# Attention and a feed-forward layer in fp32 on one core: the instruction plan redrafted with other transfer times and another table of moved works

## The chip, the cores and the metric

The kernel runs on one core of one Trainium2 chip. The metric is the device time of one execution in microseconds (us). Engines are named as the profile names them: PE multiplies matrices (PEld is its weight load), DVE and ACT do the elementwise work, SP issues every DMA; POOL only sets constants at the start.

## The reference, cut to what matters

```python
scores = scale * np.matmul(q, k.transpose(0, 1, 3, 2))          # 4 batches, 12 heads, 448 tokens, head size 64
scores = np.where(mask, -1000000000.0, scores)                  # causal
attn = np.exp(scores - np.max(scores, axis=-1, keepdims=True))
attn = attn / (np.sum(attn, axis=-1, keepdims=True) + 1e-09)
x = np.matmul(attn, v)                                          # then 1792 tokens x 768
...
h = x @ w_in                                                    # 768 -> 2048, w_in and w_out are float64
g = np.where(h > 0.0, h, np.exp(np.minimum(h, 0.0)) - 1.0)
return (g @ w_out).astype(np.float32)                           # 2048 -> 768
```

## The kernel before, in words

Attention goes by pairs of heads: 6 pairs for each of 4 batches. A pair's scores (L534, tile `sc`) are reduced to a masked, shifted block on DVE (L439, tiles `a` and `nm`), exponentiated on ACT (L443, with the row sums `su`), transposed on PE (L565, tile `tr`), copied out by ACT (L569) or DVE (L570, tile `at`), and multiplied with `v` on PE (L584, tile `av`). The sums become reciprocals on DVE (L448 and L449, tile `rr`). For the first two pairs of batch 0 the reciprocals `rr_80` and `rr_81` are spread over the partitions by PE (L604, tile `rb`) and copied by ACT (L871, tile `rs`); later ones go through a small DRAM round trip (`rdram`, `R`). DVE multiplies `av` with them (L608 or L466) into x.

The weights come as float64 bit patterns. Each piece of w_in (`w64`, 768 KB, L696) is turned into fp32 by five steps: DVE L704, ACT L708, DVE L709, ACT L712, DVE L715. It is then split into a high and a low part (`whl`: the high part on ACT L743 or DVE L744, the low part on DVE L746). A product of two such split operands is three matmuls (L785 to L787, hi·hi, hi·lo, lo·hi). The first two pieces of w_in are used unsplit (L808). The second batch group and most of the output layer use sums and differences of blocks (L751), so that seven block products do for eight.

The order of all of this is not that of the program text. Every step is recorded as a work with its engine (or two possible engines), a cost, a due time and what it reads and writes. `Plan.draft` then goes through time with a small model: it keeps one clock for each engine, a time `moved` until which the DMA engines are taken, and for each work the time at which it ends; at each turn it lets the earliest engine take, among the works that could start by then, the one that is wanted first. A work's wanted time is its due time less its entry in a table of numbers, `SOONER`, by the work's number: a positive entry makes it wanted earlier, a negative one later. `Plan.run` issues the instructions in the order that comes out. All engines work through their queues in that order, and real semaphores hold them back where something is not ready; the model's times only set the order.

For a transfer the model says when its data are there. Before, that is the end of the bytes' own time plus `LANDS`, 3.2, for a transfer that is issued after `CALM`, 75.0, and plus 1.3 for one issued earlier.

Of the kernel before, what the change touches and what calls it, by code (L numbers as in the profile page):

```python
# [108 lines left out]
class Plan:  # L109
# [9 lines left out]

    SOON = 20.0  # L120

    CALM = 75.0

    FAR, QUEUE = 1e9, 2.0

# [5 lines left out]
    def add(self, ways, reads=(), writes=(), due=None, size=0.0, hold=(), after=None):  # L131
# [24 lines left out]
        return w  # L156

    SOONER = {
# [50 lines left out]
    }  # L209

    def rank(self):
# [17 lines left out]
    def draft(self, shift):  # L229
# [14 lines left out]
        moved = 0.0  # L244
        ready = {w: 0.0 for w in self.works if not w.missing}
        order = []
        while len(order) < len(self.works):
            starts = {}
            for w, t in ready.items():
# [19 lines left out]
                for way, (eng, cost, _, port) in enumerate(w.ways):  # L269
                    s = max(t, free.get(eng, 0.0))  # L270
                    if w.size and w.want > s + self.FAR:
                        s = max(s, moved - self.QUEUE)
                    if port:
                        s = max([s] + [f for e, f in ported.items() if e != eng])
# [15 lines left out]
            s, _, _, way, w = min((c for c in cands if c[0] <= s0 + 0.12), key=lambda c: (c[1], c[2]))  # L290
            _, cost, fn, port = w.ways[way]
# [5 lines left out]
                    b.ring.order.append(b)  # L297
            free[eng], w.eng = s + cost, eng
            if w.size:
                moved = max(moved, s + cost) + w.size  # L300
                w.end = moved + (self.LANDS if s > self.CALM else 1.3)
            else:
                w.end = s + cost
            order.append((w, way, s, w.end))
# [886 lines left out]
```

## Time and profile before

| what | value |
|---|---|
| median of 3 runs | 602.02 us (600.16 to 603.22) |
| the profiled execution, its own time | 599.75 us |
| its span, first to last instruction | 598.0 us |
| PE, PEld, DVE, ACT busy share of the span | 98%, 87%, 86%, 73% |
| mean granted clock of PE | 0.994 of full speed |

The span and the 1.75 us around it make the profiled time. A busy PE means that a matmul is somewhere in its pipe; so a gap in PE is a true wait, but a busy PE may still be slowed. "Granted clock" is the share of PE's full clock: 1.00 is 2.4 GHz, 0.5 is 1.2 GHz.

### The profile page before, as it was taken

The page shows a single profiled execution, that of the slowest core. Times are in us where ns is not written, and L with a number is a line of the kernel's source. Part 1 is how long each engine was busy: PE and PEld are TensorE (multiplying, and loading weights), DVE is VectorE, ACT ScalarE, POOL GpSimd, SP SyncE. Part 2 cuts the span into 40 slices and gives each one's busy share as a digit, 9 for nine tenths or more (in the row PEclk, how much of TensorE's full clock was granted, in tenths as well). Part 3 has the DMA queues.
Part 4 walks back from the last instruction along what each step waited for, and adds up shares of the span by engine and source line. Part 5 has one row for each costly group of instructions (what it writes and reads, how often), then busy time and mean ns, then how long its engine had stood idle before and what let it go on. Part 6 is the DMA issues. An engine that isn't in the chain of part 4 may idle for free.

```text
span 598.0 us, 11375 instructions
## 1 busy us (share of the span) xinstructions
PE 586.7 (98%) x4010; PEld 519.4 (87%) x4010; DVE 515.3 (86%) x1234; ACT 435.8 (73%) x998; POOL 1.5 (0%) x12
## 2 busy tenths in 40 slices
PE   7799999999999999999999999999999999999998
PEld 4677798989889888888889989999999999999997
DVE  5698899998989899999998897999778999999452
ACT  6899999998888988998777876247464758764410
POOL 0000000000000000000000000000000000000000
PEclk9799999999999999999999999999999999999999
DMA  8995977768779999897456478999733242353112
GB/s 232 408 269 167 305 219 264 214 207 224 229 230 334 359 327 317 269 292 220 136 134 222 122 253 300 336 319 315 249 85 131 80 140 98 95 161 100 36 62 76
DMA packets 81976, 127.58 MB, mean 213 GB/s; under 512 B 9472, under 2 KB 58112, under 8 KB 81920
## 3 DMA queue, kind: packets, MB, share of 16 engines
q1 hardware_dynamic: 81920, 126.87, 67.0%
q8 instruction: 31, 0.51, 0.4%
q14 instruction: 25, 0.20, 0.1%
HBM read 94.63 MB, written 32.21 MB: 212 GB/s over the span
## 4 chain that ended last, share of the span: by engine, by line
PE 82%; DVE 9%; DMA 4%; ACT 2%; issue 1%; SPq 1%; DVEq 0%; ACTq 0%
PE hp L785 12%; PE hp L787 11%; PE hp L786 11%; PE op L785 10%; PE op L786 10%; PE op L787 10%; PE av L584 6%; PE tr L565 6%; PE sc L534 5%; DVE a L439 2%; DVE whl L746 2%; DVE G L751 1%; DMA w<-in_w_in 1%; DMA k<-in_qk 1%; PE hp L808 1%
## 5 line engine op out<-in xcount | busy, mean ns | idle before, releaser
L743 ACT ACTIVATE whl<-w 128x768 fp32r<-128x768 f32 x105 | 87.6, 838 | 64.6 <-PE op L787 31.3
L785 PE MATMUL op<-ph,whl 128*128 128x448 f32 (+1 forms) x338 | 125.4, 371 | 0.0
L786 PE MATMUL op<-pl,whl 128*128 128x448 f32 (+1 forms) x338 | 123.5, 365 | 0.1
L787 PE MATMUL op<-ph,whl 128*128 128x448 f32 (+1 forms) x338 | 123.4, 365 | 0.0
L443 ACT ACTIVATE a<-a,nm 112x448 f32<-112x448 f32 (+3 forms) x192 | 99.5, 522 | 30.6 <-DVE nm L439 30.4
L746 DVE TENSOR_TENSOR whl<-w,whl 128x768 fp32r<-128x768 f32 x111 | 104.3, 951 | 3.4 <-ACT whl L743 2.8
L439 DVE CUSTOM_DVE_ANT_0 a<-sc,mask 112x112 f32<-112x112 f32 (+3 forms) x192 | 76.2, 443 | 13.2 <-PE sc L534 12.9
L785 PE MATMUL hp<-xh,whl 128*128 128x448 f32 x180 | 70.3, 390 | 0.0
L785 PEld LDWEIGHTS op<-ph,whl 128*128 128x128 f32 x338 | 63.5, 188 | 5.9 <-issue 0.3
L786 PEld LDWEIGHTS op<-pl,whl 128*128 128x128 f32 x338 | 63.6, 188 | 5.6 <-DVE pl L746 1.0
L787 PEld LDWEIGHTS op<-ph,whl 128*128 128x128 f32 x338 | 63.5, 188 | 5.5 <-DVE whl L746 0.5
L787 PE MATMUL hp<-xh,whl 128*128 128x448 f32 x180 | 65.9, 366 | 0.4 <-DVE whl L746 0.4
L786 PE MATMUL hp<-xl,whl 128*128 128x448 f32 x180 | 65.8, 365 | 0.0
L785 PE MATMUL hp<-ph,whl 128*128 128x448 f32 x168 | 61.5, 366 | 0.0
L787 PE MATMUL hp<-ph,whl 128*128 128x448 f32 x168 | 61.4, 365 | 0.0
L786 PE MATMUL hp<-pl,whl 128*128 128x448 f32 x168 | 61.3, 365 | 0.0
L565 PEld LDWEIGHTS tr<-ident,a 112*112 112x112 f32 x480 | 50.0, 134 | 10.2 <-issue 3.1
L565 PE MATMUL tr<-ident,a 112*112 112x112 f32 x480 | 57.6, 263 | 0.0
L569 ACT ACTIVATE at<-tr 112x448 f32<-112x448 f32 x114 | 55.4, 536 | 3.0 <-PE tr L565 2.9
L584 PEld LDWEIGHTS av<-at,v 112*64 112x64 f32 x960 | 46.6, 138 | 6.5 <-issue 2.5
L584 PE MATMUL av<-at,v 112*64 112x112 f32 x960 | 51.7, 263 | 0.0
L746 DVE TENSOR_TENSOR pl<-G,ph 128x448 fp32r<-128x448 f32 x64 | 38.4, 617 | 3.9 <-ACT ph L743 3.6
(92 smaller groups left out, 941.6 us busy)
## 6 DMA issues: line engine op xcount, KB each, us to landing
w<-kin SPq DMA_DIRECT2D x41, 384.0 KB, 4.9
w<-in_w_in SPq DMA_DIRECT2D x16, 768.0 KB, 7.8
w<-in_w_out SPq DMA_DIRECT2D x24, 512.0 KB, 5.9
w<-sout SPq DMA_DIRECT2D x32, 384.0 KB, 3.8
w<-kout SPq DMA_DIRECT2D x24, 384.0 KB, 3.8
kin<-w SPq DMA_DIRECT2D x16, 384.0 KB, 6.0
sout<-w SPq DMA_DIRECT2D x12, 512.0 KB, 6.6
sin<-w SPq DMA_DIRECT2D x16, 384.0 KB, 3.9
```

Of the source, the lines that this page charges most:

```text
L439: plan.add(dve(n, lambda: nc.vector.tensor_tensor_reduce(out=a()[:, c], in0=sc()[:, c], in1=mask[:, S - n:], op0=ALU.add, op1=ALU.min, sca ...
L443: plan.add(act(n, lambda: nc.scalar.activation(a()[:, c], a()[:, c], AF.Exp, bias=nm()[:, x:x + 1], scale=-1.0, accum_out=su()[:, x:x + 1] ...
L534: nc.tensor.matmul(sc[half]()[:, lo:lo + n], q(d, x, i), k(d, y, n), start=j == 0, stop=j == len(split) - 1,)
L565: nc.tensor.transpose(tr()[:, chunk(x)], group["a"][half]()[:, chunk(x)], ident)
L569: act(w, lambda: nc.scalar.activation(at()[:, :w], tr()[:, :w], AF.Copy)),
L584: nc.tensor.matmul(av()[half_of(half), chunk(i)], u["v"]()[:, half, c], at()[:, chunk(x)], start=c == 0, stop=c == i,)
L743: act(n, lambda: nc.scalar.activation(h(), x(), AF.Copy), 0.09),
L746: sub = lambda eng: lambda: eng.tensor_tensor(out=l(), in0=x(), in1=f32(h()), op=ALU.subtract)
L751: two = lambda eng: lambda: eng.tensor_tensor(out=out(), in0=x(), in1=y(), op=op)
L785: nc.tensor.matmul(acc(), wh(k), xh(), start=first, stop=False, skip_group_check=more)
L786: nc.tensor.matmul(acc(), wh(k), xl(), start=False, stop=False, skip_group_check=more)
L787: nc.tensor.matmul(acc(), wl(k), xh(), start=False, stop=last, skip_group_check=more)
```

## The change

The model's transfers are described anew, and the table is another one. While the model's `moved` is before `BEGIN`, 14.0, a transfer's bytes take 1.35 times as long (`SLOWLY`); and every transfer lands `LANDS`, 3.2, after them, early or late. No work is added or taken away, and no size, buffer or cost of a work changes. The table has about as many entries as before, with other works and other numbers (its rows are cut here to one each). From line 302 on, lines of the changed kernel have a number that is higher by one (L704 before is L705 now).

```diff
-    CALM = 75.0
+    BEGIN, SLOWLY = 14.0, 1.35
...
     SOONER = {
-        21: -18.2, 27: -21.4, 29: -6.9, 32: 10.2, 37: -12, 56: 40.2, 62: -13.4, 85: -30.9, 106: 45.5,
+        12: -55.9, 54: -74.4, 55: -11.4, 87: -3.7, 88: 96.4, 91: -8.2, 93: -22.7, 105: 26.2, 131: -16.6,
...
             if w.size:
-                moved = max(moved, s + cost) + w.size
-                w.end = moved + (self.LANDS if s > self.CALM else 1.3)
+                moved = max(moved, s + cost)
+                moved += w.size * (self.SLOWLY if moved < self.BEGIN else 1.0)
+                w.end = moved + self.LANDS
             else:
                 w.end = s + cost
```

Three places of the order that comes out follow. **Place A** is DVE, near the start, where the first pieces of w_in are met; `w_156`, `w_159` before and `w_134`, `w_136` now are the first and the second of them, and L439 is the softmax step for the second pair of heads. Before:

```order
L704 TENSOR_SCALAR w<-w_156 128x768
L704 TENSOR_SCALAR w<-w_159 128x768
L439 ISA a,nm<-sc,mask 112x336
...
L439 ISA a,nm<-sc,mask 112x112
...
L448 TENSOR_SCALAR rr_81<-su 112x8
L449 RECIPROCAL rr_81<-rr_81 112x8
L704 TENSOR_SCALAR w<-w_163 128x768
L608 TENSOR_TENSOR xf<-av,rs 128x448
```

And now:

```order
L705 TENSOR_SCALAR w<-w_134 128x768
L440 ISA a,nm<-sc,mask 112x336
...
L440 ISA a,nm<-sc,mask 112x112
...
L449 TENSOR_SCALAR rr_81<-su 112x8
L450 RECIPROCAL rr_81<-rr_81 112x8
L705 TENSOR_SCALAR w<-w_136 128x768
L609 TENSOR_TENSOR xf<-av,rs 128x448
```

The step on the second piece of w_in now stands behind the four softmax steps and the two on `rr_81`, not ahead of them.

**Place B** is PE in the same stretch, from the products of the first pair on. Before:

```order
L584 MATMUL av<-at,v 64x112 x20
L565 MATMUL tr<-ident,a 112x112 x8
L604 MATMUL rb<-ident,rr_81 64x112 x8
L534 MATMUL sc<-k_108,q_106 112x224 x2
L534 MATMUL sc<-k_120,q_110 112x224 x2
L565 MATMUL tr<-ident,a 112x112 x8
L584 MATMUL av<-at,v 64x112 x20
L565 MATMUL tr<-ident,a 112x112 x8
L534 MATMUL sc<-k_120,q_110 112x448 x2
```

And now:

```order
L585 MATMUL av<-at,v 64x112 x20
L535 MATMUL sc<-k_108,q_106 112x224 x2
L535 MATMUL sc<-k_112,q_110 112x224 x2
L566 MATMUL tr<-ident,a 112x112 x8
L605 MATMUL rb<-ident,rr_81 64x112 x8
L566 MATMUL tr<-ident,a 112x112 x16
L585 MATMUL av<-at,v 64x112 x20
L535 MATMUL sc<-k_112,q_110 112x448 x2
```

The four scores of width 224 moved ahead of the eight transposes and of `rb`, and two groups of eight transposes now stand together behind `rb`.

**Place C** is PE late in the attention, where the weights of another column block of the first layer come into use: `whl_3083` before, `whl_3349` now. Before:

```order
L786 MATMUL hp_3039<-xl_2289,whl_2901 128x448
L787 MATMUL hp_3039<-xh_2279,whl_2901 128x448
L565 MATMUL tr_3093<-ident_66,a_2977 112x112 x4
L565 MATMUL tr_3094<-ident_66,a_2978 112x112 x4
L785 MATMUL hp_3115<-xh_1191,whl_3083 128x448
```

And now:

```order
L788 MATMUL hp_3276<-xh_2262,whl_3239 128x448
L566 MATMUL tr_3316<-ident_66,a_3196 112x112 x4
L566 MATMUL tr_3317<-ident_66,a_3197 112x112 x4
L535 MATMUL sc_3332<-k_2874,q_2881 112x224
L535 MATMUL sc_3333<-k_2874,q_2881 112x224
L535 MATMUL sc_3332<-k_3047,q_3038 112x224
L535 MATMUL sc_3333<-k_3047,q_3038 112x224
L566 MATMUL tr_3361<-ident_66,a_3200 112x112 x4
L566 MATMUL tr_3362<-ident_66,a_3201 112x112 x4
L786 MATMUL hp_3384<-xh_1204,whl_3349 128x448
```

The new column block now begins behind sixteen transposes and four scores, where it began behind eight transposes.

## Rows read from the trace of the kernel before

**Rows 1.** The profile's page: busy times of the engines, and PE's clock in 40 slices.

```profile
PE 586.7 (98%) x4010; PEld 519.4 (87%) x4010; DVE 515.3 (86%) x1234; ACT 435.8 (73%) x998; POOL 1.5 (0%) x12
...
PEclk9799999999999999999999999999999999999999
```

**Rows 2.** Busy us by stretch: stretch, its length, engines (instructions), PE clock, DMA share, GB/s.

```profile
20.00:30.00 10.00, 6.68 (x55) 5.27 (x55) 8.64 (x31) 7.50 (x21) 0.00 (x0) 0.66 1.02 402
30.00:60.00 30.00, 29.48 (x285) 21.33 (x281) 26.57 (x88) 28.73 (x78) 0.00 (x0) 1.00 0.77 219
60.00:100.00 40.00, 40.00 (x330) 33.70 (x329) 36.35 (x101) 39.84 (x91) 0.00 (x0) 1.00 0.83 268
100.00:200.00 100.00, 100.00 (x795) 89.33 (x793) 91.54 (x259) 90.99 (x225) 0.00 (x0) 1.00 0.79 245
200.00:220.00 20.00, 19.55 (x145) 17.03 (x144) 17.63 (x52) 16.88 (x41) 0.00 (x0) 1.00 1.02 329
250.00:350.00 100.00, 99.86 (x733) 89.17 (x733) 95.93 (x241) 78.45 (x192) 0.00 (x0) 1.00 0.65 193
350.00:500.00 150.00, 150.00 (x831) 138.00 (x831) 130.01 (x236) 88.23 (x169) 0.00 (x0) 1.00 0.66 213
```

**Rows 3.** Who waited for whom: us in total, times, longest us.

```profile
DVE w L704 <- DMA w<-in_w_in: 6.0, 2, 3.9
...
PE rb L604 <- DVE rr L449: 3.3, 1, 3.3
```

**Rows 4.** Timeline of DVE, 18 to 24 us: start, us, instruction, [idle before <- its end].

```profile
18.57 0.56 DVE L704 TENSOR_SCALAR w<-w 128x768 f32<-128x768 f32 x1 [3.92 <-DMA w<-in_w_in]
21.26 0.56 DVE L704 TENSOR_SCALAR w<-w 128x768 f32<-128x768 f32 x1 [2.12 <-DMA w<-in_w_in]
21.73 0.50 DVE L439 CUSTOM_DVE_ANT_0 a<-sc,mask 112x336 f32<-112x336 f32 x1
...
23.17 0.20 DVE L449 RECIPROCAL rr<-rr 112x8 f32<-112x8 f32 x1
```

**Rows 5.** Timeline of ACT at the same place.

```profile
22.27 0.57 ACT L443 ACTIVATE a<-a,nm 112x336 f32<-112x336 f32 x1 [2.44 <-DVE nm L439]
```

**Rows 6.** Timeline of PE, 14 to 44 us.

```profile
14.24 0.99 PE L604 MATMUL rb<-ident,rr 112*64 112x112 f32 x16
...
23.52 1.76 PE L604 MATMUL rb<-ident,rr 112*64 112x112 f32 x16 [3.32 <-DVE rr L449]
25.21 1.84 PE L534 MATMUL sc<-k,q 64*112 64x224 f32 x8
26.98 1.74 PE L565 MATMUL tr<-ident,a 112*112 112x112 f32 x8
28.65 2.55 PE L584 MATMUL av<-at,v 112*64 112x112 f32 x40
31.13 0.98 PE L565 MATMUL tr<-ident,a 112*112 112x112 f32 x8
...
36.50 2.14 PE L584 MATMUL av<-at,v 112*64 112x112 f32 x40
...
42.13 1.01 PE L534 MATMUL sc<-k,q 64*112 64x224 f32 x8
```

**Rows 7.** The chain of work that ended last, 218 to 220 us: start, us, what.

```profile
218.80 0.88 DVE whl L746
...
219.73 0.47 PE hp L787
```

**Rows 8.** The page's costliest groups: line, engine, shapes, count | busy us, mean ns | idle before.

```profile
L743 ACT ACTIVATE whl<-w 128x768 fp32r<-128x768 f32 x105 | 87.6, 838 | 64.6 <-PE op L787 31.3
...
L443 ACT ACTIVATE a<-a,nm 112x448 f32<-112x448 f32 (+3 forms) x192 | 99.5, 522 | 30.6 <-DVE nm L439 30.4
L746 DVE TENSOR_TENSOR whl<-w,whl 128x768 fp32r<-128x768 f32 x111 | 104.3, 951 | 3.4 <-ACT whl L743 2.8
...
L569 ACT ACTIVATE at<-tr 112x448 f32<-112x448 f32 x114 | 55.4, 536 | 3.0 <-PE tr L565 2.9
```

98 rows, old and new, of the table SOONER are left out of this document.

## The prediction

> **What bounds the kernel now.** I read the busy times first. PE is busy for 586.7 of 598.0 us [rows 1], so the whole span holds 11.3 us in which PE does nothing, and the plan changes none of PE's 4010 instructions. A new order can therefore win only what PE loses by waiting, or by running at its lower clock. The clock row has one low slice, the second, and none later [rows 1].
>
> The table of stretches shows which engine sets the pace where. From 20 to 30 us PE is busy for 6.68 of 10 us at a granted clock of 0.66 [rows 2]: the one bad stretch. From 30 to 100 us ACT is busy for 28.73 + 39.84 = 68.57 of 70 us, so ACT sets the pace there, although PE also looks full. From 100 to 200 PE is busy all the time, with DVE and ACT at 91%; from 200 to 220 PE loses 0.45 us; from 250 to 350 it loses 0.14 us [rows 2]. Behind 100 us, then, PE is the bound, with DVE close behind.
>
> The waits name the cause of the bad stretch. PE waits once, 3.3 us, for the reciprocal `rr` of DVE, and DVE waits twice, 6.0 us, for pieces of w_in to land [rows 3]. The timeline joins the two: DVE stands 3.92 us until the first piece is there at 18.57 us, does L704, stands 2.12 us for the second piece until 21.26, and only then does the four softmax steps and the two steps on `rr_81`, which ends at 23.17 + 0.20 = 23.37 us [rows 4]. PE's `rb` begins at 23.52 [rows 6], and ACT has stood 2.44 us for the same softmax steps [rows 5]. Two engines wait for work that was ready, because a transfer that is not needed yet is ahead of it in DVE's queue.
>
> **The change part by part.** *The amount of work.* By the printed orders no matmul, DMA or DVE step is added or lost. Some steps change between ACT and DVE: ACT's high-part splits of 768 columns go from 105 to 101, its copies L569 from 114 to 116, with a few narrower splits both ways. At 838 and 536 ns [rows 8] that takes 4 x 0.84 - 2 x 0.54 = 2.3 us from ACT (a little less with the narrow ones) and gives DVE as many steps, out of 435.8 and 515.3 us [rows 1]. Spread over 600 us and hidden under PE, I cost it at 0; if its cover went it would be worth 2 us either way.
>
> *Place A, DVE.* The first piece of w_in has the same place on SP, with the same sixteen loads ahead of it, so I let it land at 18.57 us again. L704 on it takes 21.73 - 21.26 = 0.47 us [rows 4], to 19.04. The softmax steps up to the end of the reciprocal take 23.37 - 21.73 = 1.64 us [rows 4], to 20.68. Then comes the second piece, which lands at 21.26 and is waited for 0.6 us instead of 2.12. So `rr_81` is there 23.37 - 20.68 = 2.7 us earlier, and ACT's 2.44 us of standing go too.
>
> *Place B, PE.* In the hole before `rb` now stand four scores and eight transposes; at full clock they take about 1.0 us each, as at 42.13 and 31.13 us [rows 6]. `rb` can follow soon after 21 us. The clock is the second part of the loss. PE did nothing for 3.32 us, and the four groups that follow, `rb`, scores, transposes and products, take 1.76 + 1.84 + 1.74 + 2.55 = 7.89 us, where the same four take 0.99 + 1.01 + 0.98 + 2.14 = 5.12 us at 2.4 GHz, at 14.24, 42.13, 31.13 and 36.50 us [rows 6]: 2.8 us lost at 1.2 GHz. With the hole filled for more than half, I expect the clock to stay up here. PE can win at most 3.3 + 2.8 = 6.1 us.
>
> The Trainium skill, page "TensorE: Matmul & The Clock Gate", section "What's actually happening", holds that the clock's ramp is worth less than 1% of a typical kernel's span and should not be fitted. The trace agrees with the size (2.8 us is 0.5% of the span), and by that rule the upper end of this term would be 3.3 us in place of 6.1; no later figure hangs on it.
>
> How much of this arrives? DVE and ACT gain 2.4 to 2.7 us, PE up to 6.1. Since ACT is full from 30 to 100 us, PE can keep no larger lead than ACT has. I take **-2.7 us**, DVE's lead, which is nearest to ACT's 2.44; the ends are -6.1 (PE's own loss, if ACT were no limit) and 0 (the lead is used up while ACT sets the pace). Behind `rb`, sixteen transposes in a row wait for exponentials just issued; PE may idle 1 to 2 us there, but ACT is then working, so I count nothing.
>
> *Place C, PE.* Before, the chain that ends last comes to PE at 219.73 us from DVE, where the low part of a weight block was made [rows 7]; PE lost 0.45 us [rows 2]. Now, from the first transposes on, ACT must copy (0.54) and split the high part (0.84), and DVE must make the low part (0.95): 2.3 us [rows 8]. PE's cover is four scores and eight transposes, about 1.0 us each as above, and two products, of which one is shown with 0.47 us [rows 7]: 2.0 to 2.9 us. That is about enough if ACT is on time; but six exponentials at 0.52 us [rows 8] stand in ACT's queue ahead of it, 3.1 us. The price lies between 0 and 3.1 us. I take **+0.9**, twice what the same wait costs now, since it is nearest to that row.
>
> *SP's queue.* The fourth to seventh pieces of w_in are now issued one q/k load sooner, and one k load goes behind them. I cost it at 0: the k load belongs to a later pair, and the pieces of w_in only come sooner. DMA's mean share of 1.02 from 20 to 30 us [rows 2] shows that the DMA engines have no spare time, so if a moved load were needed at once, it would cost one more wait of the kind that DVE has now, 2.12 us [rows 4].
>
> *The end.* From 350 to 500 us PE is busy for 150.00 of 150 us with DVE at 87% [rows 2], and the last 25 rows of PE's printed order read alike before and now; DVE's and SP's steps there are shuffled, under PE's cover: 0. Were the cover gone, a wait like the one at place C, 0.45 us, would show.
>
> Sum: -2.7 + 0.9 = -1.8 us. The profiled execution took 599.75 us, 1.75 of it around the span; it becomes 597.95. It stood 2.27 below the median of the runs, 602.02, so I forecast a median of 602.02 - 1.8 = **600.2 us**.
>
> **The rivals.**
>
> *Nothing arrives.* The lead of 2.7 us is gone by 100 us or is paid back at place C (its upper price, 3.1, exceeds it). For it: ACT's work is the same within 2 us, and it was the bound for 70 us; a landing time also differs from run to run, and where the second piece lands early the old order has no hole. Against it: ACT's 2.44 us of standing lie just ahead of its full stretch, and that is the time that such a stretch gives back. Time: 602.0. Chance 0.22.
>
> *Everything arrives.* PE keeps its full 6.1 us and pays 0.9 at place C: -5.2, 596.8. For it: from 30 us on PE is hardly ever seen to wait. Against it: ACT at 98%. Chance 0.20.
>
> *Slower: a new hole of the old kind.* At place C PE waits for the low part of `whl_3349`, and its clock falls as it did at 20 us. The price is that of the old loss, 6.1 us, less the lead of 2.7: +3.4, 605.4. It decides from the point at which the wait exceeds the lead, 2.7 us, or at 2 us if the clock falls with it. For it: six exponentials in front, and DVE at 96% from 250 us on [rows 2]. Against it: the same hand-over costs 0.45 us now. Chance 0.13.
>
> *The change does not do what it says.* The table could have made an order that merely differs. Place A speaks against it: the wait for the second piece is moved off the softmax. I count this within the first rival.
>
> **How the numbers follow.** My forecast, a net gain between 0.5 and 3.3 us, has 0.45; the others have 0.22, 0.20 and 0.13. The three runs lie within 1.9 below and 1.2 above their median, so each case has some 1.5 us around it. The bound of 0.5%, about what a measurement of this kernel can tell from no change, is 3.0 us. Faster by more than it are most of "everything arrives" (0.17) and the edge of my own case (0.10): 0.27. Slower by more than it is most of the last rival (0.10), with 0.01 for scatter: 0.11. The rest, 0.62, is within it. The range reaches from 597.0, which holds half of "everything arrives", to 603.7, which leaves out most of the slow rival.
>
> **What would show it.** Right: DVE's wait for w_in falls from 6.0 to about 4.5 us, the reciprocal `rr_81` ends near 20.7 us, the hole ahead of `rb` shrinks below 2 us, and from 20 to 30 us the granted clock stays near 1.0; from 30 to 100 us ACT remains full; PE's loss at place C is about 1 us. Wrong: the second clock slice stays low, or a later slice falls; PE waits over 2.7 us for a `whl`; or DVE meets another early transfer that has not landed. If the low clock moves to the stretch just behind 30 us, place B's sixteen transposes are the cause.

## The result, and the profile after

The changed kernel takes a median of **597.08 us** (596.43 to 597.11, four runs), and the kernel before took 602.19 us beside it (600.16 to 603.22): ratio 0.9917, with a 95% interval of 0.989 to 0.9943. Timed again later it took 597.50 us (596.69 to 599.78, ten runs) against 601.68, ratio 0.9937 [0.9917, 0.9957]. The forecast was 600.2 us. The gain is 4 to 5 us, more than twice the 1.8 us that I forecast, and most of it comes from steps that the forecast did not name.

The profiled execution took 597.11 us, with a span of 595.3 us. Its page, busy times, clock in 40 slices and the chain that ended last:

```profile
PE 585.1 (98%) x4010; PEld 518.4 (87%) x4010; DVE 516.5 (87%) x1236; ACT 434.9 (73%) x996; POOL 1.5 (0%) x12
...
PEclk9989999999999999999999999999999999999999
...
PE 91%; ACT 5%; DVE 2%; DMA 0%; issue 0%; SPq 0%; DVEq 0%
```

Against [rows 1] PE is busy for 1.6 us less, and its idle time is 595.3 - 585.1 = 10.2 us instead of 11.3. The low clock slice has not gone: it has moved from the second to the third. DMA's share of the chain rounds to 0%.

The stretches that answer to [rows 2] (stretch, length, engines, PE clock, DMA share, GB/s):

```profile
20.00:30.00 10.00, 8.99 (x108) 6.99 (x104) 9.42 (x35) 10.00 (x30) 0.00 (x0) 1.00 1.02 402
30.00:60.00 30.00, 29.39 (x268) 21.13 (x270) 27.15 (x85) 29.80 (x76) 0.00 (x0) 0.94 0.83 259
60.00:100.00 40.00, 40.00 (x323) 33.96 (x320) 37.84 (x109) 39.87 (x102) 0.00 (x0) 1.00 0.79 242
220.00:250.00 30.00, 28.73 (x233) 24.95 (x232) 28.66 (x78) 27.13 (x63) 0.00 (x0) 1.00 0.92 299
```

PE loses 1.01 us from 20 to 30 us instead of 3.32, at full clock; from 30 to 60 ACT is busy for 29.80 us instead of 28.73; from 220 to 250, at place C, PE loses 1.27 us.

Who waited for whom, answering to [rows 3]:

```profile
DVE w L705 <- DMA w<-in_w_in: 4.1, 2, 3.7
...
PE hp L788 <- DVE whl L747: 1.1, 1, 1.1
PE tr L566 <- ACT a L444: 1.0, 1, 1.0
```

DVE's wait for w_in falls from 6.0 to 4.1 us, PE's wait for `rr` is gone, and two waits of about 1 us are new. The timeline of DVE and PE in this stretch, answering to [rows 4] and [rows 6]:

```profile
20.41 0.20 DVE L450 RECIPROCAL rr<-rr 112x8 f32<-112x8 f32 x1
...
21.44 0.99 PE L605 MATMUL rb<-ident,rr 112*64 112x112 f32 x16
22.36 1.75 PE L566 MATMUL tr<-ident,a 112*112 112x112 f32 x16
...
23.24 0.57 DVE L705 TENSOR_SCALAR w<-w 128x768 f32<-128x768 f32 x1
...
28.97 0.57 PE L566 MATMUL tr<-ident,a 112*112 112x112 f32 x4 [0.55 <-DVE xf L609]
30.56 1.25 PE L566 MATMUL tr<-ident,a 112*112 112x112 f32 x8 [1.02 <-ACT a L444]
```

The reciprocal of `rr_81` ends at 20.61 us, PE has no gap ahead of `rb`, and the clock is full. The sixteen transposes of place B follow at 22.36 us without a gap. PE's next two gaps, 0.55 and 1.02 us, are ahead of later transposes. The third piece of w_in is met at 23.24 us, behind four more softmax steps, and is not waited for.

So the picture at place A is the one that was forecast. The experiments ask whether it is also the cause.

### The profile page after: what moved, and what is told of

It reads as the page before. It is cut to its first block, busy times and chain, and to the rows that moved or that the text cites. A ratio compares the mean times of both kernels' runs of the same rounds, so it can differ in the third digit from the quotient of the medians.

```text
span 595.3 us, 11387 instructions
## 1 busy us (share of the span) xinstructions
PE 585.1 (98%) x4010; PEld 518.4 (87%) x4010; DVE 516.5 (87%) x1236; ACT 434.9 (73%) x996; POOL 1.5 (0%) x12
## 4 chain that ended last, share of the span: by engine, by line
PE 91%; ACT 5%; DVE 2%; DMA 0%; issue 0%; SPq 0%; DVEq 0%
PE op L786 12%; PE hp L786 12%; PE op L787 12%; PE op L788 11%; PE hp L788 11%; PE hp L787 11%; PE av L585 7%; PE sc L535 7%; PE tr L566 6%; ACT a L444 3%; PE hp L809 2%; ACT at L570 1%; ACT w L709 1%; DVE a L440 1%; DMA k<-in_qk 0%; DVE w L716 0%
## 5 line engine op out<-in xcount | busy, mean ns | idle before, releaser
L744 ACT ACTIVATE whl<-w 128x768 fp32r<-128x768 f32 x101 | 83.9, 840 | 53.6 <-PE op L788 36.5
L444 ACT ACTIVATE a<-a,nm 112x336 f32<-112x336 f32 (+3 forms) x192 | 99.8, 529 | 25.2 <-DVE nm L440 24.8
L440 DVE CUSTOM_DVE_ANT_0 a<-sc,mask 112x448 f32<-112x448 f32 (+3 forms) x192 | 76.0, 444 | 12.3 <-PE sc L535 12.3
L566 PEld LDWEIGHTS tr<-ident,a 112*112 112x112 f32 x480 | 49.4, 133 | 10.2 <-ACT a L444 2.8
L566 PE MATMUL tr<-ident,a 112*112 112x112 f32 x480 | 56.4, 260 | 1.6 <-ACT a L444 1.0
L585 PE MATMUL av<-at,v 112*64 112x112 f32 x960 | 52.9, 265 | 0.5 <-ACT at L570 0.4
L882 ACT ACTIVATE m<-hp 128x448 f32<-128x448 f32 x56 | 29.9, 541 | 25.1 <-PE hp L788 15.7
```

The costliest lines, as they stand in the source:

```text
L440: plan.add(dve(n, lambda: nc.vector.tensor_tensor_reduce(out=a()[:, c], in0=sc()[:, c], in1=mask[:, S - n:], op0=ALU.add, op1=ALU.min, sca ...
L444: plan.add(act(n, lambda: nc.scalar.activation(a()[:, c], a()[:, c], AF.Exp, bias=nm()[:, x:x + 1], scale=-1.0, accum_out=su()[:, x:x + 1] ...
L566: nc.tensor.transpose(tr()[:, chunk(x)], group["a"][half]()[:, chunk(x)], ident)
L585: nc.tensor.matmul(av()[half_of(half), chunk(i)], u["v"]()[:, half, c], at()[:, chunk(x)], start=c == 0, stop=c == i,)
L744: act(n, lambda: nc.scalar.activation(h(), x(), AF.Copy), 0.09),
L882: plan.add(act(S, lambda: nc.scalar.activation(m(), h(), AF.Relu, scale=-1.0), 0.14), [h], [m])
```

## The experiments

Most edits move single works in the finished order, with one helper:

```python
def put(order, n, after=None, before=None):
    x = next(o for o in order if o[0].n == n)
    order.remove(x)
    k = next(k for k, o in enumerate(order) if o[0].n == (before if after is None else after))
    order.insert(k + (before is None), x)
    return order
```

In the diffs, `order` is what `draft` returned, and the numbers are those of works. A work moved on one engine leaves the other queues as they are. The kernel before was run beside each of the three sets: 601.85 us (27 runs), 601.68 (33) and 602.38 (26). All ratios are to it.

### Place A alone, and the change without it

My theory was that DVE's lead of 2.7 us at place A reaches the end; its rivals were that the lead is used up on the way, and that the gain lies elsewhere in the new order. A repeat of the kernel before shows the scatter.

> The kernel before, unchanged, to see a second profile of it: its runs lay between 600.2 and 603.2 us and its first profile stood at 599.75, below their median. Theory 1 (what the change wins beyond the 2.6 us between the two profiled executions is lost near the start, where the landing of the first pieces of w_in differs from run to run): a profile near 602 us, whose DVE waits for w_in are longer than 6.0 us in sum and whose reciprocal rr_81 ends later than 23.37 us, by about as much as the run is longer. Theory 2 (the rest is lost later, by transfers that come late to a plan that counted on them): the start as in the first profile within 0.5 us, and the extra 2 us in several waits behind 40 us.

Measured: 602.64 us, 1.0015 [0.9995, 1.0036]. Its profile, of a run of 602.56 us, begins as the first one did: DVE waits 6.3 us for w_in (6.0 in the first) and `rr_81` ends at 23.58 us (23.37). What this run is longer by lies behind 40 us, as theory 2 had it. Then place A alone, in the kernel before: work 259 is L704 on the second piece of w_in, 61 the reciprocal of `rr_81`.

```diff
+        put(order, 259, after=61)
```

> The kernel before with place A alone: the DVE step on the second piece of w_in moved behind the reciprocal rr_81, nothing else. Theory 1 (the lead of 2.7 us at place A reaches the end): rr_81 ends near 20.7 us, the granted clock from 20 to 30 us is near 1.0, and the time falls by 2 to 3 us against the kernel before, ratio 0.995 to 0.997. Rival (the lead is used up by 100 us because another engine or the DMA stream sets the pace there): rr_81 just as early, but the time the same within 0.8 us, ratio 0.999 to 1.001.

Measured: 602.22 us, 1.0016 [0.9997, 1.0035]. In its profile the step does all that it should (DVE and PE at place A; `rb` stood at 23.52 in [rows 6]):

```profile
19.99 0.20 DVE L449 RECIPROCAL rr<-rr 112x8 f32<-112x8 f32 x1
...
20.34 0.99 PE L604 MATMUL rb<-ident,rr 112*64 112x112 f32 x16 [0.29 <-DVE rr L449]
...
22.61 0.56 DVE L704 TENSOR_SCALAR w<-w 128x768 f32<-128x768 f32 x1 [1.29 <-DMA w<-in_w_in]
23.08 0.62 DVE L608 TENSOR_TENSOR xf<-av,rs 128x448 f32<-128x448 f32 x1
```

In the first profile of before the step that is now at 23.08 us stood here:

```profile
23.72 0.62 DVE L608 TENSOR_TENSOR xf<-av,rs 128x448 f32<-128x448 f32 x1
```

PE is three microseconds ahead at `rb`, and nothing of it is left in the time. DVE ends `rr_81` 23.37 - 20.19 = 3.2 us earlier, but its next step but one meets the third piece of w_in before it has landed and stands 1.29 us; the step behind it is 0.6 us ahead. Next, the changed kernel with place A undone (259 ahead of the softmax steps again):

```diff
+        put(order, 259, before=88)
```

> The changed kernel with place A undone alone: the DVE step on the second piece of w_in stands ahead of the four softmax steps again. Theory 1: rr_81 ends near 23 us again, PE waits over 2 us for it, and 2 to 3 us of the gain are gone: 599 to 600 us, ratio 0.996 to 0.997 against the kernel before. Rival: 597 us as the changed kernel, ratio 0.990 to 0.993; the gain is made elsewhere in the order.

Measured: 598.38 us, 0.9957 [0.9939, 0.9975]. In its profile `rr_81` ends at 23.04 us again and PE waits 1.69 us for it, yet most of the gain stays. Last, the changed kernel with the step on the first piece, 275, behind the reciprocal too:

```diff
+        put(order, 275, after=61)
```

> The changed kernel with the DVE step on the first piece of w_in, too, moved behind rr_81. DVE's wait of 3.75 us for its landing then has softmax steps in it. Theory 1: rr_81 ends near 18.5 to 19 us, ACT's and PE's work follows earlier, and the time falls by another 1 to 2 us to about 595.5, ratio 0.987 to 0.990. Rival (leads from the start are used up later): 597 us, ratio 0.990 to 0.993.

Measured: 597.57 us, 0.9949 [0.9929, 0.9969]. No further gain; but the edit made no further lead either. DVE no longer waits for w_in, but it waits 2.43 us for an exponential of ACT instead, and `rr_81` ends at 20.58 us (20.61 in the changed kernel, 18.5 to 19 expected). So this run says nothing of what a larger lead is worth.

So place A alone is worth nothing in the old order. In the new one it is worth about 1 us (598.38 against 597.08 and 597.50 us; 2.4 by the furthest pair of ratios, 0.9957 and 0.9917), which is not clear of the noise: the intervals overlap. The theory falls.

### Which part of the order

The next set cuts the order in time: the first works from one order, then the works that are left in the sequence of the other. Theory E puts the gain into the first 60 us, theory L behind them. The edit for a cut at 60 us, where `now` is the changed order and `old` that of before (1091 in place of 318 cuts at 190 us; for the reverse, 320 works of `old` come first):

```diff
+        head = now[:318]
+        seen = {o[0] for o in head}
+        order = head + [o for o in old if o[0] not in seen]
```

> The changed kernel again, unchanged, to stand in one comparison with the mixed orders. Both theories: its median lies near 597.1 us, ratio to the kernel before 0.989 to 0.995, and its runs scatter less than those of before.

That is the changed kernel, unchanged. Measured: 597.50 us, 0.9937 [0.9917, 0.9957].

> The reverse: the order of before for the first 320 works (the first 60 us), then the rest in the changed order. Theory E: the first hole and the low clock are back, no gain: 600.5 to 602.5. Theory L: the scatter narrows and most of the gain is there, 597.5 to 599.5, though PE's clock is low from 23 to 29 us as before.

Measured: 602.46 us, 1.0024 [1.0004, 1.0043]. The new order from 60 us on gives nothing by itself, as theory E had it.

> The changed order for the first 1091 works (some 190 us), then the rest in the order of before. Theory E: the same as with the cut at 60 us, 598.5 to 599.5. Theory L: if the waits that come and go lie between 60 and 190 us, 597 to 598.5; if they lie behind 190 us, where PE waits for low parts of weights in the old order, 600.5 to 602. In either theory place C of the changed order (1.1 us at about 230 us) is gone from its profile.

Measured: 598.72 us, 0.9953 [0.9932, 0.9975]: most of the gain is made in the first 190 us.

> The changed order for the first 318 works (the first 60 us or so), then the works that are left in the order of before. Theory E (the gain is made in the first 60 us: fewer waits of PE from 20 to 60 us): it keeps most of the gain, -2.6 to -3.4 us, median 598.5 to 599.5. Theory L (the gain comes later, from waits that the old order meets in some runs only): median 601 to 602.5, no more than 1 us below before.

Measured: 600.68 us, 0.9995 [0.997, 1.0021], with runs from 598.11 to 605.60. The median is nearer to theory L's number, the spread is neither's, and its profile, taken of the slowest run, shows why (DVE and PE behind the seam):

```profile
68.19 0.56 DVE L525 TENSOR_TENSOR xf<-av,R 128x384 f32<-128x384 f32 x1 [4.89 <-DMA R<-rdram]
...
69.83 1.71 PE L624 MATMUL tr<-ident,a 112*112 112x112 f32 x8 [4.90 <-DVE nm L498]
```

(Lines of the mixed kernels are numbered higher; L525 is L466.) At the seam the old order takes up the product with `R` too soon behind its load: DVE stands 4.89 us, the softmax steps behind it wait, and PE with them. So this cut does not decide between the two theories. The seam made this wait, but it pointed to the real question: who waits for `R` in the two orders?

### The round trip of R

From the third pair of heads on the reciprocals go through DRAM: DVE spreads them (`tt`, L482), SP stores them (`rdram<-tt`), SP loads them back in two parts (`R<-rdram`), DVE multiplies (L466). In the repeat of the kernel before, whose profiled run took 602.56 us, near its median, the chain of waits from 38 to 62 us runs right through it:

```profile
39.97 3.96 DMA rdram<-tt
...
43.94 0.58 SPq L488
...
44.58 5.00 DMA R<-rdram
...
49.65 0.56 DVE xf L466
50.21 0.53 DVE a L439
...
50.80 1.55 PE sc L534 x7
```

For 3.96 + 5.00 = 9.0 us the chain is two transfers, of 16 and 128 KB. The timeline of DVE and PE in the same run:

```profile
32.24 0.21 DVE L482 STREAM_TRANSPOSE tt<-rr 128x32 f32<-128x32 f32 x1
39.37 0.21 DVE L482 STREAM_TRANSPOSE tt<-rr 128x32 f32<-128x32 f32 x1
45.60 0.69 DVE L466 TENSOR_TENSOR xf<-av,R 128x384 f32<-128x384 f32 x2 [0.96 <-DMA R<-rdram]
...
49.65 0.56 DVE L466 TENSOR_TENSOR xf<-av,R 128x384 f32<-128x384 f32 x1 [0.35 <-DMA R<-rdram]
...
50.80 1.55 PE L534 MATMUL sc<-k,q 64*112 64x336 f32 x8 [1.38 <-DVE nm L439]
```

and its stretch from 40 to 60 us (columns as in [rows 2]), in which PE loses 1.38 us and ACT 1.11:

```profile
40.00:60.00 20.00, 18.62 (x168) 13.18 (x165) 16.96 (x58) 18.89 (x50) 0.00 (x0) 1.00 0.69 188
```

The same timeline and stretch of the changed kernel:

```profile
27.17 0.21 DVE L483 STREAM_TRANSPOSE tt<-rr 128x32 f32<-128x32 f32 x1
35.49 0.21 DVE L483 STREAM_TRANSPOSE tt<-rr 128x32 f32<-128x32 f32 x1
43.48 0.65 DVE L467 TENSOR_TENSOR xf<-av,R 128x384 f32<-128x384 f32 x2
...
49.74 0.55 DVE L467 TENSOR_TENSOR xf<-av,R 128x384 f32<-128x384 f32 x1
```

```profile
40.00:60.00 20.00, 20.00 (x196) 15.05 (x198) 17.36 (x54) 19.93 (x50) 0.00 (x0) 1.00 0.72 222
```

From the spread to the product the old order leaves 45.60 - 32.24 = 13.4 us for the first of these pairs, waits included, and 49.65 - 39.37 = 10.3 us for the second. The new one leaves 43.48 - 27.17 = 16.3 and 49.74 - 35.49 = 14.3 us, and neither of these products waits. The new constants are of a size to explain it: the model lets a transfer issued before 75 us land 3.2 - 1.3 = 1.9 us later, and the round trip is two transfers, so 3.8 us. No run had the new constants without the new table, so this is argued and not shown. Drafts of the order that were not run speak for it: with the table of before, the new constants put the first product five steps later in DVE's queue; with the old constants, the new table puts it eleven steps sooner.

SP plays a part too: the old order has the next pair's store between the two loads of `R`, and issues them at 39.17 and 40.56 us; the new one issues both together, at 35.85.

The lead of place A meets the same step, in the timeline of DVE with place A alone:

```profile
44.21 0.69 DVE L466 TENSOR_TENSOR xf<-av,R 128x384 f32<-128x384 f32 x2 [1.31 <-DMA R<-rdram]
```

In the first profile of before:

```profile
44.93 0.69 DVE L466 TENSOR_TENSOR xf<-av,R 128x384 f32<-128x384 f32 x2 [0.31 <-DMA R<-rdram]
```

DVE got there at 44.21 - 1.31 = 42.90 us instead of 44.62, 1.7 us ahead, and left the wait 0.7 us ahead. At the fourth of these products it stood again, 0.87 us, and began it at 65.19 us, where the first profile has 64.87: the lead is gone. In `old_to_60` the same step stood 2.21 us. This made theory W, that the waits for `R` use up what the old order wins elsewhere. The last set tests it in both directions. First the kernel before, with the steps that meet transfers moved later (119, 120 and 150 are products with `R`, 121 and 122 the splits behind them, 325 and 326 the products of batch 1, 558 a step L704 that waits for its buffer) and the second load of `R`, 114, moved sooner on SP, next to the first:

```diff
+        put(order, 114, after=113); put(order, 119, after=367); put(order, 120, after=119)
+        put(order, 121, after=120); put(order, 122, after=121); put(order, 150, after=370)
+        put(order, 325, after=343); put(order, 326, after=325); put(order, 558, after=433)
```

> The order of before, with the early DVE steps that meet a transfer moved a little later, and nothing else: the first product with R behind three softmax steps and one L715, the second behind four steps, the first one of batch 1 behind two reciprocal steps, one L704 that waits for a buffer behind four steps, and one R load on SP moved ahead of the next pair's store. Place A is not touched. Theory W (the old order loses its time from 30 to 85 us in waits for the round trip of R, because those steps stand too soon behind their transfers): DVE's waits for R before 85 us, 1.7 to 2.5 us, are gone and the median falls by 0.5 to 1.5 us, to 600.3 to 601.3. Theory U (these waits lie under ACT's full queue): 601.3 to 602.3.

Measured: 599.12 us, 0.9956 [0.9931, 0.9981], a gain of 3.3 us, more than expected. Then the same with place A:

```diff
+        put(order, 259, after=61)
```

> The same later steps, and place A as well (L704 on the second piece of w_in behind the reciprocal of rr_81). Place A alone gave nothing. Theory W (its lead was used up in waits for R): now the lead arrives, 2.5 to 3.5 us below before, 598.3 to 599.3. Theory U: no more than 1 us below before, 600.8 to 602.

Measured: 599.47 us, 0.9962 [0.994, 0.9983]: 2.9 us, which is theory W's number for both edits, but place A adds nothing to the first one, and that part of theory W falls. In this profile the third piece of w_in is waited for 1.27 us and the products with `R` 1.5 us in all (1.0 in that of `old_r_later`). Against that profile `rr_81` ends 2.2 us earlier, the spread at 30 us is 0.35 us earlier, and the first product with `R` is 0.25 us later, so the lead is used up there. Then the reverse edit, on the changed kernel, with the same load of `R` put back behind the next pair's store:

```diff
+        put(order, 114, after=140); put(order, 119, before=181)
+        put(order, 120, after=119); put(order, 150, before=215)
```

> The changed kernel with the reverse edit: the first product with R put four softmax steps and more sooner, the second one sooner by four steps, and one R load behind the next pair's store, as before. All else as changed. Theory W: DVE waits for R by 1.5 to 3 us between 40 and 52 us where it waited for nothing, and the median rises by 1 to 2.5 us, to 598.3 to 600. Theory U: 597 to 598.

Measured: 601.66 us, 0.9975 [0.9958, 0.9992]. Putting the products back loses 4.0 us against `new_c_sooner` of the same set, whose early part is the changed kernel's (2.3 us by the ratio to `a_again`'s 0.9937): what theory W expected, or more. Its profile, of its quickest run, shows the wait return, DVE's and then PE's:

```profile
42.31 0.69 DVE L467 TENSOR_TENSOR xf<-av,R 128x384 f32<-128x384 f32 x2 [1.87 <-DMA R<-rdram]
...
43.05 1.00 PE L535 MATMUL sc<-k,q 64*112 64x448 f32 x2 [1.10 <-DVE xf L467]
```

Moving a handful of steps gives the old order most of the gain, and moving the like steps back takes 2.3 to 4.0 us from the new one. Two limits belong to this. First, a single profile does not carry it: the profile of `old_r_later` still has 1.0 us of waits for `R`, and of the 3.7 us that it gains on the repeat of before it has gained 1.9 at the spread at 30 us, ahead of the edit, by a full clock; the verdict rests on the medians. The gain also holds at equal clock: among runs whose mean granted clock was above 0.995, the kernel before has a median of 600.85 us (30 runs), place A alone 601.86 (8), `old_r_later` 598.83 (6). The loss is halved there: `new_r_sooner` has 599.52 us (5) against 597.67 for `new_c_sooner` (6), 1.8 us; its other seven runs had a clock of 0.993 or 0.994, and where it was lost was not profiled. Second, the edit of `old_r_later` bundles three products, a buffer wait and an R load that stood behind the next pair's store; which of them carries most was not tried. The buffer wait is no small part: in the repeat of before it is 1.41 us, the two early waits for `R` are 0.96 + 0.35 = 1.31. `new_r_sooner` leaves out the buffer wait and one product, so those are not the whole of it; the R load is in both edits. That the steps' places carry most of the gain is shown; that the waits for `R` themselves do is only the likeliest reading.

The new order is not proof against it: in the profile of `a_first_piece` a product waits 2.3 us for `R`, and PE loses 1.5 us behind it. Nor does each such wait cost time: in the changed kernel's own profile two products of later batches wait 2.4 us for `R`, at 322 and 391 us, while PE is busy throughout (15.00 of 15 us from 315 to 330 and from 385 to 400).

### Place C

The changed kernel, with the low part of the weight block, work 1323, ahead of L705 and the softmax steps:

```diff
+        put(order, 1323, before=1423)
```

> The changed kernel with place C mended: the low part of the weight block (DVE L747) that PE waits for at 235 us goes ahead of L705 and of three softmax steps, 1.3 us of DVE's work. If place C's price reaches the end: PE's wait of 1.1 us is gone and the median falls by 0.7 to 1.2 us, to 596.0 to 596.8. If it is hidden by later waits: within 0.4 us of 597.3.

Measured: 597.67 us (six runs), 0.9923 [0.99, 0.9945], the same as the changed kernel. PE's wait for `whl` is gone, and another of the same size stands a little later:

```profile
239.50 0.47 PE L786 MATMUL op<-ph,whl 128*128 128x448 f32 x1 [1.12 <-ACT ph L744]
```

From 220 to 250 us PE still loses 30 - 28.69 = 1.3 us. It looks as if DVE and ACT were behind PE here, so that the wait falls on whatever PE asks for next; no run shows more than this one exchange. No version was quicker than the changed kernel.

## Why the prediction was right or wrong

*The bound and the bad stretch* were read rightly. Each local sign came: `rr_81` at 20.61 us (20.68 forecast), DVE's wait for w_in at 4.1 (4.5), no hole ahead of `rb`, clock 1.00 from 20 to 30 us, ACT busy for 69.67 of 70 us from 30 to 100.

*The number* lay inside the stated range, but only just: 597.08 us, where the range begins at 597.0. Since the gain was not made on the sum's path, that is luck.

*Place A, "I take -2.7 us, DVE's lead",* is the step that failed. I had reasoned that ACT's standing time lies ahead of its full stretch and would be given back. Alone it measures 1.0016 [0.9997, 1.0035]; in the new order it is worth about 1 us, not clear of the noise. In the profile of `b_place_a` the lead runs into the next early transfers: 1.29 us at the third piece of w_in, then 1.31 and 0.87 us at the round trip of `R`, and by 65 us it is gone. The changed kernel meets the third piece four softmax steps later and does not wait for it. I had named "another early transfer that has not landed" as a sign of being wrong, but looked for none; in the profile of before the wait for `R` was 0.31 us, and I passed over it because I read ACT's 68.57 of 70 us as a full engine. In the repeat ACT is busy for 18.89 of 20 us from 40 to 60, and the 1.11 us that it lacks are two waits for DVE's steps behind those for `R`.

*The change of the constants* got no term of its own. I treated the diff as a cause of places A, B and C, and did not ask which transfers are in use before 75 us and what 1.9 us more for each does to their users. That term, not in my sum, is -3.3 us by `old_r_later`, buffer wait included, and 1.8 to 4.0 us the other way by `new_r_sooner`.

*Place B, counted at 0,* held, but my sign for it was wrong. I had expected PE to idle at the sixteen transposes behind `rb`, and had tied a low clock just behind 30 us to them. They run at 22.36 us without a gap. The low clock does come there, 0.51 from 31.9 to 35.4 us, behind the gaps of 0.55 and 1.02 us ahead of later transposes. But those gaps alone do not bring it: in `new_c_sooner` they are 0.28 and 1.27 us, and the clock stays at 1.00 from 30 to 40 us. The cost is small: of the first four runs two had a mean clock of 1.0 (596.43 and 597.04 us) and two 0.997 (597.11 both). The Trainium skill's page "TensorE: Matmul & The Clock Gate", section "What's actually happening", holds that the ramp's penalty is below 1% of a typical kernel's span. The groups of runs by mean clock, at the end of this text, lie at most 0.4% apart, which agrees in size; the groups may differ in their waits too.

*Place C, +0.9,* was close as PE's wait, 1.1 us. As a price it is not shown: with that wait taken away the time stayed the same, and PE waited as long 4 us later.

*The rivals.* "Nothing arrives" was right of place A's lead. "Everything arrives" gave almost the measured time, 596.8 us, for a reason that did not hold: most of PE's 6.1 us at `rb` was won in `b_place_a` too (a gap of 0.29 us, and a full clock from 20 to 30 us) and did not last. No new hole of the old kind appeared: PE's longest wait for a `whl` was 1.1 us.

*The base.* I summed against an execution of 599.75 us, which lay 2.3 below the median. The pair of first profiles differs by 2.64 us, the medians by 5.1, so a profile that happens to be of a quick run can hide half of the difference. The repeat of before, 2.8 us longer, shows a part of what was hidden: PE loses 0.9 us more than in the first profile from 40 to 60 us, and 0.7 us more from 100 to 250 us.

## What to carry to other kernels

A lead won on one engine can be spent where its next steps meet a transfer; follow the chain onward to the next DMA before you count it. A wait for a transfer of 0.3 us in one profile marks a step without slack; here the same step waited 0.96 us in the next profile. Look at the scatter of the runs, too (598.6 to 604.8 us over the 86 runs of before in the three sets, 596.4 to 599.8 over the 14 of the changed kernel). Where a planner orders the work, a landing time that is too short counts twice on a round trip.

## What the runs showed of the hardware

A store with a 48th of the bytes of a load of w_in took two thirds of that load's time to land in one kernel, and nine tenths in the other. The rows are DMA issues from 30 to 60 us, their count, KB each and median us from issue to landing, of the repeat of before:

```profile
w<-in_w_in SPq DMA_DIRECT2D x3, 768.0 KB, 5.2
...
rdram<-tt SPq DMA_DIRECT2D x4, 16.0 KB, 3.5
```

and of the changed kernel:

```profile
w<-in_w_in SPq DMA_DIRECT2D x4, 768.0 KB, 6.5
...
rdram<-tt SPq DMA_DIRECT2D x3, 16.0 KB, 5.8
```

The 16 KB store takes 3.5 and 5.8 us where DMA's mean share is 0.7 to 1.0. The Trainium skill, page "DMA: Bandwidth & Descriptors", section "Anatomy of one DMA — SWDGE (gpsimd) path", fits 2.0 us and the bytes at 436 GB/s for one DMA on another path; an estimate from it would be 2.04 us for this store. The measurement is 1.5 to 3.8 us longer on SP's queue among other loads, so here a planner needs the landing time of its own stretch.

The mean granted clock of one kernel also differs between executions. Of the 86 runs of before, 30 had more than 0.995 (median 600.85 us), 36 had 0.994 (601.92) and 20 had 0.991 to 0.993 (603.46). Which stretch is slow in the last was not profiled.
